# Attention and two MLP blocks on one core: narrower weights for the low half of P·V, and P·V products set between transposes

## The chip, the cores and the metric

The kernel runs on 1 core of one Trainium2 chip (trn2). The metric is the device time of one execution in microseconds (us). The kernel before takes 672.0 us (median of 3 runs, 671.81 to 672.73).

The engines are named as in the profile: PE is TensorE (matmul), PEld its weight load, DVE is VectorE, ACT is ScalarE, POOL is GpSimd, SP the engine that issues the DMAs. PE reads a stationary operand (the weights, loaded beforehand) and a moving operand from SBUF and writes to PSUM.

## The reference

An attention with a mask by hash buckets is followed by two dense blocks:

```python
mask = q_bucket[:, :, :, None] == k_bucket[:, :, None, :]       # 6 sign bits of q @ proj, k @ proj
scores = scale * np.matmul(q, k.transpose(0, 1, 3, 2))          # 2 x 8 heads, 768 x 768, head size 64
scores = np.where(mask, scores, -1000000000.0)
scores = scores - np.max(scores, axis=-1, keepdims=True)
attn = np.exp(scores)
attn = attn / (np.sum(attn, axis=-1, keepdims=True) + 1e-09)
return np.matmul(attn, v).astype(np.float32)
...
zr, zi = x * cos(x @ w_theta), x * sin(x @ w_theta)             # second block
u = x + w_tok_r @ zr + w_tok_i @ zi;  x = u + relu(u @ w_ch)
...
x + relu(layernorm(x) * g_ln @ w_ch1) @ w_ch2                   # third block
```

All is float32. The change touches the attention alone, in its product of the normalised P (`attn`) with V.

## The kernel before

**Halves.** A float32 factor is split into a high half, which PE multiplies exactly enough in its fast 32-bit form (fp32r), and a low half, the rest. A product is then made of several matmuls whose sum is accumulated in PSUM.

**Steps.** The 16 heads have 768 rows of scores each. One unit of work `p` is 256 rows of a head (two tiles of 128 rows, called a and b), so there are 48 units. For a unit the stages are:

- `Sa`, `Sb` (`s_mm`, L316): scores of tile a and b, four matmuls each, into a PSUM tile that has one buffer for a and one for b.
- `Ma`, `Mb` (`s_max`, L325): DVE takes the row maximum. `Ea`, `Eb` (`s_exp`, L343): ACT makes the exponentials p and their sums l. `R1`, `R2` (L353, L357): POOL and DVE make 1/l. `na`, `nb` (L361): POOL scales, which gives pn.
- `U0`, `U1`, `U2` (`p_transpose`, L374): PE transposes the twelve 128x128 blocks of pn, four to a PSUM bank (T0, T1, T2).
- `H0` to `H2` (L383): ACT copies a bank of four transposed blocks to pth, which rounds them to the high half. `L0` to `L2` (L101): DVE subtracts, which gives the low half ptl.
- `PV` (`pv_mm`, L399): twelve matmuls, six with pth and six with ptl as moving operand (256 columns). The weights are 128 columns of vv: the 64 columns of V's high half beside the 64 of its low half. So rows 0 to 63 of the result hold P times V high and rows 64 to 127 hold P times V low. They go to the bank `O`, of which there is one.
- `O` (`pv_evac_a`, L408): ACT copies rows 64 to 127 to ot. `X` (`pv_evac_b`, L417): DVE adds rows 0 to 63 and ot into xT. The next unit may write the bank O only after `X`.

**Order.** The order in which the instructions of each engine stand is written out by hand. The first units are in a list (`head`). From step k = 8 on, the list `plan` is gone through once a step; its number is how many units an operation lags, so step k holds `Sa` of unit k, `U0` to `U2` of unit k-2 and `PV` of unit k-3. Each engine does its part of that list in order, and waits in place where something is not ready. In four steps (k = 19 to 22) `plan_b` is used instead. It also makes the hash bits of four pairs of heads: `B1`, eight matmuls on PE (L272); `B2`, a copy on ACT (by, L288); `B3`, a comparison on DVE (bb, L294); `B4` on POOL. In `plan_b`, `U2` stands ahead of `U1`, and DVE's `X` stands behind `B3`. The text calls these the four bits steps, and the others plain steps.

`G`, `C` and `D` in the lists are places for background work of that step (splitting K, Q and V into halves, converting weights). `C` is ACT's: copies `hiq`, `hik` (L196) and `vv` (L94) of 128x384. For the V of a pair of heads, `v_steps` says in which step it is loaded and in which two steps its halves are made; POOL follows one step later with V's low half.

A last list (`tail`) holds the last units and the start of the second block.

Of the kernel before, what the change touches and what calls it, by code (L numbers as in the profile page):

```python
# [33 lines left out]
def attn_moe_kernel(  # L34
# [18 lines left out]
    NI = S // 128  # L53
# [9 lines left out]
    vec, act, pool, pe, sp = nc.vector, nc.scalar, nc.gpsimd, nc.tensor, nc.sync  # L63
# [7 lines left out]
    def bank(tag, name):  # L71
        return psum.tile([128, 512], F32, tag=tag, name=name)
# [6 lines left out]
    ident = const.tile([128, 128], F32, name="ident")  # L79
# [132 lines left out]
    vv_t = {}  # L212
# [78 lines left out]
    def bits_b_(pairs, nm, hf):  # L291
        n = pairs[0], nm, hf
        b = ap_.tile([64, HALF], F32, name="bb", **bits_tag(pairs, nm, hf))
        vec.scalar_tensor_tensor(  # L294
            out=b, in0=bits_ps.pop(n)[0:64], scalar=-1.0, in1=bits_y.pop(n), op0=ALU.mult, op1=ALU.is_lt
        )
        bits_b[n] = b

    def bits_p_(pairs, nm, hf):
        n = pairs[0]  # L300
        b = bits_b.pop((n, nm, hf))
        r0 = 0 if nm == "q" else 64
        pool.tensor_scalar(
            out=halves(bits_t[n][r0:r0 + 64], hf), in0=b, scalar1=mulb[nm], scalar2=addb[nm],
            op0=ALU.mult, op1=ALU.add,
        )

    s_ps, m_t, p_t, pn_t, l_t = {}, {}, {}, {}, {}
# [58 lines left out]
    pt_t = {}  # L367
    t_ps = {}
# [19 lines left out]

    o_ps = {}

    def pv_mm(p):
        h = p // (NI // 2)
        n, e = divmod(h, 2)
        vv = vv_t[n]
        ps = bank("O", f"o{p}")[:, 0:256]
        k = 0
        for x in pt_t.pop(p):
            for c in range(NI):
                pe.matmul(  # L399
                    ps, vv[:, c, e].rearrange("p a d -> p (a d)"), x[:, c::NI, :],  # L400
                    start=(k == 0), stop=(k == 2 * NI - 1),
                )
                k += 1
        o_ps[p] = ps

    def pv_evac_a(p):
        t = ap_.tile([64, 256], F32, tag="ot", bufs=3, name=f"ot{p}")
# [19 lines left out]
    def theta_steps(c, x):  # L427
# [18 lines left out]

    plan = (
# [3 lines left out]
    )  # L451

    plan_b = (
# [4 lines left out]
    )  # L458

# [77 lines left out]
    def at(step, fn, *args):  # L537
        bg.setdefault(step, []).append((fn, args))
# [8 lines left out]
    for h in range(5, B * H):  # L547
        at({8: 20}.get(h, 3 * h - 7), stack_dma, h)
        at({8: 21, 9: 21}.get(h, 3 * h - 7), stack_bits, h)
    v_steps = {2: (6, 9, 10), 3: (15, 16, 18), 4: (20, 22, 23)}  # L550
    for n in range(2, NPAIR):
        ld, *hi = v_steps.get(n, (6 * n - 6, 6 * n - 3, 6 * n - 2))
        at(ld, load_v, n)
# [12 lines left out]
    for i in range(8):  # L566
        c, x = divmod(i, 2)
# [31 lines left out]
    def run_bg(q):  # L599
# [10 lines left out]
        "R1": s_guard, "R2": s_recip, "na": lambda p: s_norm(p, 0), "nb": lambda p: s_norm(p, 1),  # L610
        "B1": lambda p: bits_chunk(*bq[p], "T1"), "B2": lambda p: bits_y_(*bq[p]),
        "B3": lambda p: bits_b_(*bq[p]), "B4": lambda p: bits_p_(*bq[p]),
        "PV": pv_mm, "O": pv_evac_a, "X": pv_evac_b,
    }
    for u in range(3):
        ops[f"U{u}"] = lambda p, u=u: p_transpose(p, u)
# [27 lines left out]
    def bp_(x, e):  # L644
# [20 lines left out]
        vh=lambda n, x: v_hi(n, act, x), vl=lambda n, x, e: v_lo(n, ve[e], x),  # L665
        D=direct_mm, Q=direct_bits, S=s_mm, M=s_max, E=s_exp, tb=s_lone, R1=s_guard, R2=s_recip,
        n=s_norm, U=p_transpose, H=p_hi, L=p_lo, PV=pv_mm, O=pv_evac_a, X=pv_evac_b,
    )

# [691 lines left out]
    last = """  # L1361
# [71 lines left out]
```

## Time and profile before

| | |
|---|---|
| median of 3 runs | 672.0 us (671.81 to 672.73) |
| the profiled execution | 672.49 us, its span 670.7 us |
| PE busy | 661.3 us, 99% of the span |
| DVE busy | 565.0 us, 84% |
| ACT busy | 417.3 us, 62% |
| POOL busy | 336.1 us, 50% |
| granted TensorE clock | 1.00 over the whole span |

The span runs from the first to the last instruction; the 1.8 us between it and the time of the execution lie outside the trace. The attention with its steps fills the first 240 us. Busy shares are means over stages that differ: in the attention three engines are each close to full, later PE alone is. Matmuls overlap in the records, since one starts while the results of the one before are still on their way to PSUM, so what a matmul costs PE is the distance of two starts and not its duration.

### The profile page before, as it was taken

Reading aid. Unit: us, or ns where it says so; the run is one execution under the profiler, and the core shown is the slowest. Engines: PE = TensorE matmul, PEld = TensorE weight load, DVE = VectorE, ACT = ScalarE, POOL = GpSimd, SP = SyncE. Lnnn points to the kernel's source line nnn. Section 1 sums busy time; section 2 is a strip of 40 time slices with the busy share of each in tenths; the row PEclk is TensorE's granted clock in tenths of the full one; section 3 lists DMA queues with packets and bytes.
Section 4 is the critical chain, followed back from the end, with each engine's and each line's share of the span. In section 5 each row is a group of like instructions: output and inputs, shape, how many; then the busy total and the mean of one; then the engine's idle time right before and its main releaser. Section 6 shows DMA issues by size and latency. Waiting matters only on the chain.

```text
span 670.7 us, 11175 instructions
## 1 busy us (share of the span) xinstructions
PE 661.3 (99%) x3766; PEld 590.0 (88%) x3766; DVE 565.0 (84%) x989; ACT 417.3 (62%) x865; POOL 336.1 (50%) x476
## 2 busy tenths in 40 slices
PE   8999999999999999999999999999999999999997
PEld 7899999999899888878888888988998988889896
DVE  6999988999999999999988888996766676767654
ACT  7899998999999897666534644554333434343321
POOL 6797888777887655342513445523241505050400
PEclk9999999999999999999999999999999999999999
DMA  8777554475542111121532113101111111220013
GB/s 247 189 169 208 138 115 113 95 182 134 129 114 89 48 47 64 47 82 45 172 110 80 47 56 102 63 1 64 63 64 64 64 64 63 77 82 32 0 48 141
DMA packets 32229, 62.23 MB, mean 93 GB/s; under 512 B 4466, under 2 KB 11460, under 8 KB 32173
## 3 DMA queue, kind: packets, MB, share of 16 engines
q1 hardware_dynamic: 32173, 61.53, 31.9%
q8 instruction: 30, 0.49, 0.3%
q14 instruction: 26, 0.21, 0.1%
HBM read 39.98 MB, written 3.15 MB: 64 GB/s over the span
## 4 chain that ended last, share of the span: by engine, by line
PE 82%; DVE 9%; POOL 3%; DMA 2%; issue 2%; ACT 1%; SPq 0%; DVEq 0%; POOLq 0%; ACTq 0%
PE o L1155 20%; PE zy L1120 12%; PE acc L840 11%; PE o L399 8%; PE t L374 8%; PE s L316 8%; PE v L1120 5%; PE a L882 5%; POOL pn L361 2%; DVE arena L101 1%; PE th L774 1%; DMA raws<-in_kT_dram 1%; PE bits L272 1%; DMA tk<-lok 1%; DVE cy L124 1%
## 5 line engine op out<-in xcount | busy, mean ns | idle before, releaser
L1155 PE MATMUL o<-arena,hh 128*128 128x512 f32 x384 | 119.7, 393 | 0.0
L361 POOL TENSOR_SCALAR pn<-p,l,M 128x768 f32<-128x768 f32 x96 | 95.0, 991 | 24.1 <-DVE l L357 16.8
L325 DVE TENSOR_REDUCE M<-s 128x1 f32<-128x772 f32 x96 | 91.1, 950 | 3.1 <-PE s L316 1.8
L101 DVE TENSOR_TENSOR ptl<-t,pth 128x512 fp32r<-128x512 f32 x144 | 90.7, 680 | 0.3 <-ACT pth L383 0.2
L343 ACT ACTIVATE p<-s,M 128x768 f32<-128x768 f32 x96 | 87.2, 908 | 5.7 <-DVE M L325 5.1
L383 ACT ACTIVATE pth<-t 128x512 fp32r<-128x512 f32 x144 | 81.8, 599 | 4.5 <-PE t L374 3.0
L316 PE MATMUL s<-tk,tq 128*128 128x386 f32 (+1 forms) x360 | 82.5, 351 | 0.0
L374 PE MATMUL t<-ident,pn 128*128 128x128 f32 x576 | 81.1, 274 | 1.1 <-DVE ptl L101 0.4
L1128 ACT ACTIVATE sn<-zy 128x384 f32<-128x384 f32 x48 | 23.6, 491 | 91.6 <-PE zy L1120 91.6
L1155 PEld LDWEIGHTS o<-arena,hh 128*128 128x128 f32 x384 | 70.5, 188 | 9.7 <-DVE arena L101 0.2
L1155 PE MATMUL o<-arena,hl 128*128 128x512 f32 x192 | 76.1, 397 | 0.0
L374 PEld LDWEIGHTS t<-ident,pn 128*128 128x128 f32 x576 | 67.6, 141 | 9.4 <-POOL M L332 2.5
L840 PE MATMUL acc<-arena,tokh 128*128 128x512 f32 x240 | 75.5, 395 | 0.0
L117 POOL TENSOR_SCALAR cs<-st 128x512 f32<-128x512 f32 (+2 forms) x65 | 41.4, 642 | 56.3 <-DVE cy L124 53.5
L316 PEld LDWEIGHTS s<-tk,tq 128*128 128x128 f32 (+1 forms) x360 | 59.3, 190 | 0.2 <-ACT vv L94 0.2
L1086 POOL TENSOR_TENSOR s<-cy 128x256 f32<-128x256 f32 x7 | 5.2, 742 | 96.8 <-DVE cy L124 96.8
L1145 DVE SCALAR_TENSOR_TENSOR hl<-c,hh 128x384 fp32r<-128x384 f32 x48 | 28.3, 591 | 28.3 <-ACT hh L1141 28.2
L840 PEld LDWEIGHTS acc<-arena,tokh 128*128 128x128 f32 x240 | 44.2, 188 | 8.9 <-DVE arena L101 0.3
L124 DVE SCALAR_TENSOR_TENSOR cy<-cy,cs 128x512 uint32<-128x512 uint32 (+2 forms) x72 | 43.6, 606 | 6.8 <-ACT cy L114 1.0
L114 ACT ACTIVATE cy<-st 128x512 f32<-128x512 f32 (+2 forms) x72 | 40.1, 561 | 11.7 <-DVE tokl L101 4.9
L840 PE MATMUL acc<-arena,tokl 128*128 128x512 f32 x120 | 46.9, 391 | 0.0
L121 DVE SCALAR_TENSOR_TENSOR cs<-st,cs 128x512 uint32<-128x512 uint32 (+2 forms) x76 | 46.2, 608 | 0.2
(233 smaller groups left out, 1555.8 us busy)
## 6 DMA issues: line engine op xcount, KB each, us to landing
st<-in_w_dram SPq DMA_DIRECT2D x36, 256.0 KB
st<-in_w_dram SPq DMA_DIRECT2D x14, 512.0 KB
tk<-hik SPq DMA_DIRECT2D x30, 193.0 KB
tq<-hiq SPq DMA_DIRECT2D x30, 192.0 KB
st<-in_wrT_dram SPq DMA_DIRECT2D x12, 384.0 KB
st<-in_wiT_dram SPq DMA_DIRECT2D x12, 384.0 KB
vs<-in_v_dram SPq DMA_DIRECT2D x8, 384.0 KB
tk<-lok SPq DMA_DIRECT2D x15, 193.0 KB
```

Of the source, the lines that this page charges most:

```text
L101: eng.tensor_tensor(out=o, in0=i, in1=f(hi), op=ALU.subtract)
L124: vec.scalar_tensor_tensor(out=yu, in0=yu, scalar=3, in1=su, op0=ALU.logical_shift_left, op1=ALU.bitwise_or)
L316: pe.matmul(ps[:, hf, 0:HW], lt[0:K, x * 128:(x + 1) * 128], rt[0:K, hf, :], start=(K == 128), stop=(K != 128),)
L325: vec.tensor_reduce(out=m_t[p][:, 0, i:i + 1], in_=s_ps[p, i][:, :, 0:HW], axis=AX.XY, op=ALU.max, negate=True)
L343: act.activation(pt, ps[:, :, 0:HALF], AF.Exp, bias=m[:, 0, i:i + 1], accum_out=l_t[p][:, 0, i:i + 1])
L361: pool.tensor_scalar(out=pn.rearrange("p c s -> p (c s)"), in0=p_t.pop((p, i)).rearrange("p c s -> p (c s)"), scalar1=l_t[p][:, 1, i:i + 1 ...
L374: pe.transpose(ps[:, w * 128:(w + 1) * 128], pn_t[p, i][:, c, :], ident)
L383: act.activation(ph, t_ps[p, u], AF.Copy)
L399: pe.matmul(ps, vv[:, c, e].rearrange("p a d -> p (a d)"), x[:, c::NI, :], start=(k == 0), stop=(k == 2 * NI - 1),)
L840: pe.matmul(acc, w[:, x, t * 128:(t + 1) * 128], z[:, x, y, :], start=(j == 0 and k == 0), stop=(j == NI - 1 and k == 5),)
L1120: pe.matmul(ps_t[r, b], W1[g][y][:, w, d, :], XB[s][x][:, z, d, :], start=(first == 1 and k == 0), stop=(k == 5), skip_group_check=True,)
L1155: pe.matmul(ps, lt[:, i * 128:(i + 1) * 128], W2[g][:, y, x, :], start=(k == 0), stop=(k == 5))
```

## The change

```diff
+    NARROW = 72
+    LOW, HIGH = range(NI, 2 * NI), range(NI)
+
+    def pv_one(p, k, first, last):
+        n, e = divmod(p // (NI // 2), 2)
+        y, c = divmod(k, NI)
+        m = NARROW if y else 128
+        pe.matmul(
+            o_ps[p][0:m], vv_t[n][:, c, e].rearrange("p a d -> p (a d)")[:, 0:m], pt_t[p][y][:, c::NI, :],
+            start=first, stop=last,
+        )
+        if last:
+            pt_t.pop(p)
+
     def pv_mm(p):
...
+        o_ps[p] = bank("O", f"o{p}")[:, 0:256]
+        ks = (HIGH[0], *LOW, *HIGH[1:])
+        for k in ks:
+            pv_one(p, k, k == ks[0], k == ks[-1])
+
+    def pv_rest(p):
+        ks = (*LOW[4:], *HIGH[1:])
+        for k in ks:
+            pv_one(p, k, False, k == ks[-1])
+
+    def pv_between(p):
+
+        q = p + 1
+        o_ps[p] = bank("O", f"o{p}")[:, 0:256]
+        ps = bank("T2", f"t{q}_2")
+        for k in HIGH[:1]:
+            pv_one(p, k, k == 0, False)
+        for w in range(4):
+            i, c = divmod(8 + w, NI)
+            pe.transpose(ps[:, w * 128:(w + 1) * 128], pn_t[q, i][:, c, :], ident)
+            pv_one(p, LOW[w], False, False)
+        t_ps[q, 2] = ps
...
     plan = (
-        ("R2", 1), ("U1", 2), ("Sb", 0), ("Mb", 0), ("H1", 2), ("U2", 2), ("Ea", 0), ("ta", 0), ("H2", 2),
-        ("G", 0), ("na", 1), ("PV", 3), ("tb", 0), ("Eb", 0), ("L0", 2), ("C", 0), ("L1", 2), ("O", 3),
+        ("R2", 1), ("U1", 2), ("Sb", 0), ("Mb", 0), ("H1", 2), ("PW", 2), ("Ea", 0), ("ta", 0), ("H2", 2),
+        ("G", 0), ("na", 1), ("PX", 3), ("tb", 0), ("Eb", 0), ("L0", 2), ("C", 0), ("L1", 2), ("O", 3),
...
-    v_steps = {2: (6, 9, 10), 3: (15, 16, 18), 4: (20, 22, 23)}
+    v_steps = {2: (6, 9, 10), 3: (15, 16, 17), 4: (20, 22, 23)}
...
+        "PV": pv_mm, "PW": lambda p: pv_between(p - 1), "PX": pv_rest, "O": pv_evac_a, "X": pv_evac_b,
```

A product with P's low half now has 72 weight columns: V's high half and 8 columns of its low half. In the head and the tail `pv_mm` still makes a unit's twelve products together, with the first high one ahead of the six low ones. In the 40 steps of `plan` and `plan_b`, `PW` stands in `U2`'s place: the first high product of unit k-3, then four times one transpose of `U2` (unit k-2) and one narrow low product. `PX` stands in `PV`'s place with the remaining two low and five high products. `plan_b` is edited in the same way.

PE in a plain step before: the transposes of `U2` (t_2) are followed by the products of unit k-3 (o). What stands in brackets is the engines whose semaphores an instruction waits for.

```order
L316 MATMUL s_1_937<-tk_581,tq_579 128x386 [waits PE_49,Activation_49]
L316 MATMUL s_1_937<-tk_581,tq_579 128x386
L316 MATMUL s_1_937<-tk_582,tq_580 128x386 x2
L374 MATMUL t_2_944<-ident,pn_1_923 128x128 [waits DVE_49]
L374 MATMUL t_2_944<-ident,pn_1_923 128x128 x3
L399 MATMUL o_973<-pth_860,vv_556 128x256 [waits DVE_49]
L399 MATMUL o_973<-pth_860,vv_556 128x256 x5
L399 MATMUL o_973<-ptl_861,vv_556 128x256 x6
```

The same place now:

```order
L316 MATMUL s_1_937<-tk_581,tq_579 128x386 [waits PE_49,Activation_49]
L316 MATMUL s_1_937<-tk_581,tq_579 128x386
L316 MATMUL s_1_937<-tk_582,tq_580 128x386 x2
L398 MATMUL o_944<-pth_860,vv_556 128x256 [waits DVE_49]
L425 MATMUL t_2_945<-ident,pn_1_923 128x128
L398 MATMUL o_944<-ptl_861,vv_556 72x256
L425 MATMUL t_2_945<-ident,pn_1_923 128x128
L398 MATMUL o_944<-ptl_861,vv_556 72x256
L425 MATMUL t_2_945<-ident,pn_1_923 128x128
L398 MATMUL o_944<-ptl_861,vv_556 72x256
L425 MATMUL t_2_945<-ident,pn_1_923 128x128
L398 MATMUL o_944<-ptl_861,vv_556 72x256 x3
L398 MATMUL o_944<-pth_860,vv_556 128x256 x5
```

The first product, which waits for DVE (for `X` of the unit before, which frees the bank O), now stands ahead of the four transposes instead of behind them.

PE in the second of the four bits steps, from the transposes of `U2` (t_2) on, before:

```order
L374 MATMUL t_2_1690<-ident,pn_1_1682 128x128 [waits DVE_49,Pool_49]
L374 MATMUL t_2_1690<-ident,pn_1_1682 128x128 x3
L374 MATMUL t_1_1698<-ident,pn_0_1640 128x128 [waits DVE_49]
L374 MATMUL t_1_1698<-ident,pn_0_1640 128x128
L374 MATMUL t_1_1698<-ident,pn_1_1682 128x128 x2
L399 MATMUL o_1708<-pth_1588,vv_1057 128x256 [waits DVE_49]
L399 MATMUL o_1708<-pth_1588,vv_1057 128x256 x5
L399 MATMUL o_1708<-ptl_1589,vv_1057 128x256 x6
```

And the same step now:

```order
L398 MATMUL o_1691<-pth_1588,vv_1057 128x256 [waits DVE_49,Activation_49]
L425 MATMUL t_2_1692<-ident,pn_1_1683 128x128 [waits Pool_49]
L398 MATMUL o_1691<-ptl_1589,vv_1057 72x256
...
L398 MATMUL o_1691<-ptl_1589,vv_1057 72x256
L374 MATMUL t_1_1706<-ident,pn_0_1641 128x128 [waits Activation_49]
L374 MATMUL t_1_1706<-ident,pn_0_1641 128x128
L374 MATMUL t_1_1706<-ident,pn_1_1683 128x128 x2
L398 MATMUL o_1691<-ptl_1589,vv_1057 72x256 x2
L398 MATMUL o_1691<-pth_1588,vv_1057 128x256 x5
```

Here eight transposes, those of `U2` and of `U1`, now stand behind the product that waits.

On ACT the order is the same but for one copy of vv (the second half of V's pair 3), which goes from the second bits step to the first. Before, from the by of the first bits step to that of the third:

```order
L196 ACTIVATE hiq_1558<-raws 128x384
L196 ACTIVATE hiq_1624<-raws 128x384 [waits DMAHW5_49,DMAHW0_49]
...
L288 ACTIVATE by<-bits 64x384 [waits PE_49]
...
L94 ACTIVATE vv_1556<-vs_1465 128x6x64
L196 ACTIVATE hiq_1624<-raws 128x384
```

And now:

```order
L94 ACTIVATE vv_1556<-vs_1471 128x6x64
L196 ACTIVATE hiq_1558<-raws 128x384
L196 ACTIVATE hiq_1631<-raws 128x384 [waits DMAHW5_49,DMAHW0_49]
...
L288 ACTIVATE by<-bits 64x384 [waits PE_49]
...
L196 ACTIVATE hiq_1631<-raws 128x384
```

So the first bits step has three such copies and the second has one, where each had two. On POOL the subtraction that goes with this copy comes one step earlier too. The orders of DVE and of SP's DMAs are as before.

## Rows read from the trace of the kernel before

**Rows 1.** The page, part 1: busy time (share of the span) and instructions.

```profile
PE 661.3 (99%) x3766; PEld 590.0 (88%) x3766; DVE 565.0 (84%) x989; ACT 417.3 (62%) x865; POOL 336.1 (50%) x476
```

**Rows 2.** Stretches: busy PE, PEld, DVE, ACT, POOL (counts), clock, DMA share, GB/s.

```profile
59.33:80.18 20.85, 20.85 (x163) 20.47 (x162) 20.39 (x36) 20.61 (x46) 18.77 (x31) 1.00 0.53 142
93.61:115.95 22.34, 22.34 (x163) 21.76 (x162) 18.59 (x33) 19.49 (x42) 18.21 (x28) 1.00 0.43 100
133.23:225.05 91.82, 91.17 (x672) 85.42 (x673) 90.69 (x163) 86.39 (x190) 72.24 (x117) 1.00 0.47 118
```

**Rows 3.** Timeline of PE, a plain step: start, us, what, count.

```profile
68.47 0.88 PE L399 MATMUL o<-ptl,vv 128*128 128x256 f32 x6
69.18 0.87 PE L316 MATMUL s<-tk,tq 128*128 128x386 f32 x4
69.89 1.04 PE L374 MATMUL t<-ident,pn 128*128 128x128 f32 x8
70.68 0.97 PE L316 MATMUL s<-tk,tq 128*128 128x386 f32 x4
71.48 0.60 PE L374 MATMUL t<-ident,pn 128*128 128x128 f32 x4
```

**Rows 4.** Timeline of DVE, the same step.

```profile
70.19 0.95 DVE L325 TENSOR_REDUCE M<-s 128x1 f32<-128x772 f32 x1
71.17 0.42 DVE L417 TENSOR_TENSOR xT<-o,ot 64x256 f32<-64x256 f32 x1
```

**Rows 5.** One line's matmuls: duration ns min/median/max, first and last start.

```profile
L374 PE MATMUL t<-ident,pn x576: 270/272/331, 20.9 to 242.1; 128*128 128x128 f32 x192
...
L399 PE MATMUL o<-pth,vv x288: 274/282/388, 30.2 to 248.2; 128*128 128x256 f32 x144
```

**Rows 6.** Timeline of PEld where P·V waits for X.

```profile
212.13 0.77 PEld L399 LDWEIGHTS o<-pth,vv 128*128 128x128 f32 x6 [0.27 <-DVE xT L417]
```

**Rows 7.** Timeline of DVE at that place.

```profile
211.66 0.42 DVE L417 TENSOR_TENSOR xT<-o,ot 64x256 f32<-64x256 f32 x1
...
214.84 0.95 DVE L325 TENSOR_REDUCE M<-s 128x1 f32<-128x772 f32 x1
```

**Rows 8.** Timeline of PE at that place.

```profile
213.66 0.87 PE L316 MATMUL s<-tk,tq 128*128 128x386 f32 x4
```

**Rows 9.** Timeline of PE, the four bits steps.

```profile
98.39 1.04 PE L374 MATMUL t<-ident,pn 128*128 128x128 f32 x8
...
100.69 0.86 PE L316 MATMUL s<-tk,tq 128*128 128x386 f32 x4
...
102.66 0.34 PE L272 MATMUL bits<-lok,pb_lo 128*128 128x384 f32 x1
...
103.99 1.04 PE L374 MATMUL t<-ident,pn 128*128 128x128 f32 x8
...
106.30 0.87 PE L316 MATMUL s<-tk,tq 128*128 128x386 f32 x4
...
117.46 0.87 PE L316 MATMUL s<-tk,tq 128*128 128x386 f32 x4
```

**Rows 10.** Timeline of DVE, the first two bits steps.

```profile
98.59 0.42 DVE L417 TENSOR_TENSOR xT<-o,ot 64x256 f32<-64x256 f32 x1
...
104.19 0.42 DVE L417 TENSOR_TENSOR xT<-o,ot 64x256 f32<-64x256 f32 x1
```

**Rows 11.** Timeline of ACT, from the first bits step to the second.

```profile
99.46 1.09 ACT L383 ACTIVATE pth<-t 128x512 fp32r<-128x512 f32 x2
100.43 0.94 ACT L196 ACTIVATE hiq<-raws 128x384 fp32r<-128x384 f32 x2
101.26 0.90 ACT L343 ACTIVATE p<-s,M 128x768 f32<-128x768 f32 x1
...
102.28 0.38 ACT L408 ACTIVATE ot<-o 64x256 f32<-64x256 f32 x1
103.04 0.49 ACT L288 ACTIVATE by<-bits 64x384 f32<-64x384 f32 x1 [0.38 <-PE bits L272]
```

More of the change, by code (lines that the diff above doesn't have):

```diff
@@ L389, in attn_moe_kernel @@
     o_ps = {}
-    def pv_mm(p):
[L392 to L404, printed above, removed]
+    NARROW = 72
[10 more added lines that the diff above has]
+            pt_t.pop(p)
+    def pv_mm(p):
+        o_ps[p] = bank("O", f"o{p}")[:, 0:256]
[17 more added lines that the diff above has]
+        t_ps[q, 2] = ps
     def pv_evac_a(p):
@@ L612, in attn_moe_kernel @@
         "B3": lambda p: bits_b_(*bq[p]), "B4": lambda p: bits_p_(*bq[p]),
-        "PV": pv_mm, "O": pv_evac_a, "X": pv_evac_b,
+        "PV": pv_mm, "PW": lambda p: pv_between(p - 1), "PX": pv_rest, "O": pv_evac_a, "X": pv_evac_b,
     }
```

4 rows, old and new, of the table plan_b are left out of this document.

## The prediction

> **What bounds the kernel now.** I read the page first. PE is busy for 99% of the span, DVE for 84% [rows 1]. That says that PE counts, but not where, so next come the stretches of the attention, since the change touches nothing else. In five plain steps (59.33 to 80.18) PE is busy all the time, DVE for 20.39 of 20.85 us and ACT for 20.61 [rows 2]: three engines are full at once, and one step takes 20.85 / 5 = 4.17 us. In the four bits steps PE is busy throughout, but DVE only for 18.59 of 22.34 us; a step takes 5.58 us and is PE's. From 133 to 225 us, 21 steps of 4.37 us on average, DVE has 90.69 of 91.82 us: there DVE is the bound. So PE work that is saved is worth at most DVE's idle time: 0.46 / 5 = 0.09 us a step early, 1.13 us in the whole late stretch.
>
> Then the timelines, for what a matmul costs PE. Six P·V products take 69.18 - 68.47 = 0.71 us, 0.12 each. Eight transposes and four score matmuls behind them take 71.48 - 69.89 = 1.59 us; the four score matmuls alone are 0.71 (69.18 to 69.89), so a transpose costs 0.88 / 8 = 0.11 [rows 3].
>
> **The change part by part.** *Narrow weights alone.* A P·V matmul lasts 282 ns, but 388 where nothing hid its weight load, so 128 columns load in 106 ns; for a transpose 331 - 272 = 59 ns [rows 5]. A load of 106 ns is hidden behind a product every 0.12 us. Where low products follow each other, a shorter load saves nothing: 0, and 0.12 stays. No row has a load of 72 columns. It lies between 0 and 106 ns if narrowing doesn't make it longer; I take 106 x 72/128 = 60 ns, close to the 59 of the nearest short load.
>
> The Trainium skill (TensorE: Matmul & The Clock Gate, "LDWEIGHTS (loading the stationary operand)") says that a load goes with its columns at 1.2 per ns, whatever the rows. That makes an estimate of 107 ns for 128 columns, which the 106 here agrees with, and 60 for 72; by it the sum below stands, and with a load that doesn't shrink, rival 1 would hold.
>
> *Pairs.* A transpose followed by anything with 128 weight columns costs 0.11, as if it waited for the 106 ns of the next load. With a 60 ns load behind it, the pair of transpose and low product should cost 0.06 + 0.12 = 0.18 instead of 0.11 + 0.12 = 0.23. The ends are 0.12 (the transpose vanishes) and 0.23 (the transpose itself holds PE). At 0.18, PE saves 4 x 0.05 = 0.19 us a step (0.44 - 0.25). In the head and tail nothing stands between: 0.
>
> *The wait that moves.* The bank O is free only when DVE has made xT. Before, that wait stood behind `U2`; now `U2` stands behind it, and in the bits steps `U1` too. The signal takes 212.13 - (211.66 + 0.42) = 0.05 us [rows 6, 7]. Then PE needs 0.11 for the unhidden load, 0.12 for the first product, 4 x 0.18 = 0.72, and seven more products, 0.83: 1.78 us until the next `Sa`.
>
> In a plain step this closes a loop: xT, signal 0.05, PE 1.78, `Sa` 0.87 until its result is there [rows 3], then DVE's maximum and xT, 71.59 - 70.19 = 1.40 [rows 4]: 4.10 us, and a signal from PE to DVE. In the rows DVE takes `Sa` 0.14 us after its end (70.05 to 70.19), though it was busy until then, so that signal is at most 0.14. The loop is 4.10 to 4.24 against 4.17 today. Where P·V already waits for xT there was more room: `Sa` ended at 214.53 and DVE came at 214.84 [rows 7, 8]; now `Sa` ends 1.78 + 0.05 - (213.66 - 212.08) = 0.25 later, still before 214.84. So PE's saving pays for the late start and no more: 0 a step. The ends are -0.07 and +0.07 in some 27 steps (40 less four bits steps, a third of the 21 late ones whose loop has room because DVE converts weights too, and two at the start); DVE's idle time allows no gain over 0.09 x 11 + 1.13 = 2.1 us. I carry -1 and +1.9.
>
> *The bits steps.* Here xT stands behind bb, which waits for ACT's by, which waits for eight bits matmuls. xT of the first ends at 99.01 [rows 10], while PE began `U2` at 98.39 [rows 9]. Now PE waits until 99.06. It then does the 1.78 us and, between, four transposes of `U1` (0.44): 2.22 us, so the next `Sa` starts at 101.28 instead of 100.69: +0.59. Queued behind the wait are `U2`, `U1`, the rest of P·V and the next scores, and ACT waits for `U1`. This now goes round:
> - PE's way: from `Sa` to by is 103.04 - 100.69 = 2.35, from by to the end of xT 104.61 - 103.04 = 1.57, signal 0.05, PE 2.22: 6.19 us a step instead of 5.58 [rows 9 to 11].
> - ACT's way: PE's last transpose of `U1` ends 0.11 + 0.12 + 0.72 + 3 x 0.11 + 0.27 = 1.55 after the wait; signal 0.03; two evictions 0.97 (99.46 to 100.43); copies at 0.83 / 2 = 0.415 each; from the exponential to ot 1.02; ot and the gap 0.41 [rows 11]. Then by.
>
> Second step: by PE's way by starts at 101.28 + 2.35 = 103.63. By ACT's it is 99.06 + 1.58 + 0.97 + 3 x 0.415 + 1.02 + 0.41 = 104.29, with three copies since one of vv moved here. The later counts: xT ends at 105.86, PE goes on at 105.91, where `U2` began at 103.99. Third: PE's way gives by at 105.91 + 2.22 + 2.35 = 110.48, ACT's, with one copy, 110.31; so PE goes on at 112.10. Fourth, no copies: 112.10 + 6.19 = 118.29. The next `Sa` is at 120.51 instead of 117.46: +3.05 us. Nothing gives it back, since DVE has only 1.13 us idle in the whole later stretch and its order is unchanged.
>
> *POOL and ACT for V.* The moved copy is counted above; POOL's subtraction (one of its late ones) falls where POOL has 22.34 - 18.21 = 4.1 us idle [rows 2]: 0. Uncovered it would delay only the next norm. DMAs keep their order and place.
>
> **Sum.** 0 for the weights, 0 (-1 to +1.9) for the plain steps, +3.05 for the bits steps: 672.49 + 3.05 = 675.5 us for an execution like the profiled one. That one stands 0.49 above the median of 672.0, so the forecast is 675.0 us, its own range 674.0 to 677.0.
>
> **Rivals.** 1. *The pairs bring nothing* (the load doesn't shrink, or a transpose holds PE for its 0.11 whatever follows). For it: a transpose's own load is 59 ns, yet transposes in a row still cost 0.11, so something other than that load sets their distance. Against it: eight transposes take only 0.79 until the next score matmul is let in (69.89 to 70.68), which then waits, so PE seems free sooner. Then each loop is 0.19 longer: the bits steps cost 3.05 + 4 x 0.19 = 3.8, and the 27 plain steps some 0.17 each, 4.6: 680.4 us.
>
> The Trainium skill (the same page, "Part 4: PE-mode transpose") says that transposes don't lift the clock as matmuls do and that one takes about 275 ns; the 272 here agrees, but the granted clock is 1.00 in all three stretches, so the trace doesn't say that the array is held. By that rule rival 1 would come.
>
> 2. *Not slower: the transposes vanish wholly* (a pair costs 0.12). For it speaks the same 0.79. Against it, the weights must still be in place, and no row shows a load under 59 ns. PE then needs 1.78 - 0.24 = 1.54, the plain loop is at most 4.00, and DVE's idle time becomes the gain: up to 2.1 us. The bits steps cost less: the first 0.59 - 0.24 = 0.35, then PE's `U1` ends 0.24 sooner, so 105.67, and two more of 5.95: 117.57 + 1.98 = 119.55 against 117.46, +2.1. Sum 0: 672.0 us. It decides from pairs under some 0.13 on; anything more that hides in the bits steps makes it faster.
>
> 3. *Late transposes stall others.* `H2` on ACT comes later where P·V waited for xT, by the moved wait; against it, ACT has 91.82 - 86.39 = 5.4 us idle in that stretch [rows 2]. If DVE's low halves then wait, 0.1 us in each of the 40 steps adds 4: 679.
>
> **Chances.** Forecast 0.58; rival 1 0.18; rival 2 0.17; rival 3 0.07. Under 0.2% (1.3 us) this kernel's runs can't be told from no change. Rival 2 lies around no change: same 0.11, faster 0.06. The rest is slower: 0.83. For 8 in 10 the range reaches from rival 2's 671.6 to 681.0 above rival 1: about 0.1 is left out in all.
>
> **What would show it.** In the profile after: low products with 72 columns 0.18 apart where a transpose lies between (0.23: rival 1, 0.12: rival 2); PEld waiting for xT in nearly all plain steps by 0.1 to 0.3 us, at unchanged 4.17 a step; four bits steps of some 6.0 to 6.8 us in place of 5.58, with PE idle by 0.7 us or more before each; the second with three copies the longest. DVE's idle time in the bits steps grows by 3 us. If the bits steps stay at 5.6, the forecast is wrong at its main term; if plain steps leave 4.17 by more than 0.1, at the loop.

## The result and the profile after

The changed kernel takes 680.55 us (median of four runs, 679.93 to 681.16); the kernel before took 672.07 beside it. The ratio is 1.012, with a 95% interval of 1.0108 to 1.0131: 8.5 us slower, where 3.0 were forecast. The number that came is the one of rival 1.

The page, part 1, and the chain of waits by engine (part 4), of the kernel after, then that chain of the kernel before:

```profile
PE 665.3 (98%) x3766; PEld 590.3 (87%) x3766; DVE 567.4 (84%) x989; ACT 419.0 (62%) x865; POOL 334.5 (49%) x476
...
PE 64%; DVE 21%; POOL 4%; issue 4%; ACT 4%; DMA 2%; SPq 1%; DVEq 0%; POOLq 0%; ACTq 0%
```

```profile
PE 82%; DVE 9%; POOL 3%; DMA 2%; issue 2%; ACT 1%; SPq 0%; DVEq 0%; POOLq 0%; ACTq 0%
```

The busy times hardly differ from [rows 1]: no engine has more work (PE's record has 4.0 us more, but it counts waits as busy, as seen below). What is new is waiting, and the chain now goes through DVE for 21% of the span, where it was 9%. Three stretches of the kernel after follow: five plain steps, the four bits steps and 21 late steps, each cut from one `Sa` to another (columns as in [rows 2]):

```profile
61.24:82.92 21.68, 21.68 (x163) 20.30 (x161) 21.09 (x36) 21.29 (x47) 19.18 (x31) 1.00 0.59 158
95.60:121.93 26.33, 23.61 (x162) 21.72 (x161) 18.55 (x32) 19.01 (x42) 18.63 (x28) 1.00 0.33 77
135.04:229.84 94.80, 91.78 (x675) 85.08 (x674) 92.20 (x162) 87.91 (x190) 72.80 (x119) 1.00 0.45 115
```

The stretches in [rows 2] were cut from one P·V to another. For the first two that makes 0.01 us of difference at most; the same 21 late steps of the kernel before, from `Sa` to `Sa`, are these:

```profile
129.98:222.00 92.02, 91.34 (x675) 85.44 (x673) 90.83 (x163) 86.54 (x190) 72.87 (x118) 1.00 0.46 118
```

The granted clock is 1.00 in all of them. A plain step takes 21.68 / 5 = 4.34 us, 0.17 more; the four bits steps 26.33 - 22.34 = 3.99 more, and PE is idle in them for 2.72 us, where it had no idle time; the 21 late steps 94.80 - 92.02 = 2.78 more. The rows of waits of the kernel after, 30 to 240 us (engine, line, what it waited for: total, times, longest), name the place:

```profile
PEld o L398 <- DVE xT L440: 9.7, 23, 0.8
ACT pth L383 <- PE t L374: 7.5, 11, 1.5
PE o L398 <- DVE xT L440: 5.4, 11, 1.0
ACT pth L383 <- PE t L425: 5.0, 14, 0.6
```

PEld waits for xT 9.7 us, in 23 of the 36 plain steps. Of PE's 5.4 us, 3.2 lie in eight of those same steps and are part of the 9.7; the other 2.2 are in three of the bits steps. So P·V waits for xT about 11.9 us in 26 steps. In the kernel before, that wait was 1.4 us in 6 steps, of which [rows 6] show one. One plain step, first on PE, then on DVE:

```profile
69.91 0.87 PE L316 MATMUL s<-tk,tq 128*128 128x386 f32 x4
...
72.28 0.39 PE L398 MATMUL o<-pth,vv 128*128 128x256 f32 x1
72.51 0.27 PE L425 MATMUL t<-ident,pn 128*128 128x128 f32 x1
72.54 0.36 PE L398 MATMUL o<-ptl,vv 128*72 128x256 f32 x1
72.74 0.27 PE L425 MATMUL t<-ident,pn 128*128 128x128 f32 x1
72.76 0.36 PE L398 MATMUL o<-ptl,vv 128*72 128x256 f32 x1
72.96 0.27 PE L425 MATMUL t<-ident,pn 128*128 128x128 f32 x1
...
74.24 0.87 PE L316 MATMUL s<-tk,tq 128*128 128x386 f32 x4
```

```profile
70.82 0.96 DVE L325 TENSOR_REDUCE M<-s 128x1 f32<-128x772 f32 x1
71.81 0.42 DVE L440 TENSOR_TENSOR xT<-o,ot 64x256 f32<-64x256 f32 x1
...
75.14 0.96 DVE L325 TENSOR_REDUCE M<-s 128x1 f32<-128x772 f32 x1
```

The pairs stand 72.74 - 72.51 = 0.23 us apart. A low product starts 0.03 us after its transpose, but lasts 360 ns where one without a transpose in front takes 280, as if it waited inside the array. The loop can be read off, link by link: xT ends at 72.23, PE goes on at 72.28, the next `Sa` starts 1.96 later (1.78 was forecast), DVE's maximum 0.90 after that, and the next xT ends 1.41 after the maximum starts: 0.05 + 1.96 + 0.90 + 1.41 = 4.32, and 74.24 - 69.91 = 4.33. PE counts as busy for all 21.68 us of the plain stretch, although it waits 0.15 to 0.33 us in each step: PEld shows that wait (20.30 us busy). In PE's record it is hidden, since the last score matmul ends only at 72.38, after the first product has started.

The second bits step of the kernel after, the longest. First ACT, then DVE:

```profile
101.38 1.09 ACT L383 ACTIVATE pth<-t 128x512 fp32r<-128x512 f32 x2 [1.42 <-PE t L374]
102.35 0.53 ACT L94 ACTIVATE vv<-vs 128x384 fp32r<-128x384 f32 x1
102.76 0.94 ACT L196 ACTIVATE hiq<-raws 128x384 fp32r<-128x384 f32 x2
103.59 0.90 ACT L343 ACTIVATE p<-s,M 128x768 f32<-128x768 f32 x1
...
104.60 0.38 ACT L431 ACTIVATE ot<-o 64x256 f32<-64x256 f32 x1
104.89 0.47 ACT L288 ACTIVATE by<-bits 64x384 f32<-64x384 f32 x1
```

```profile
99.07 0.42 DVE L440 TENSOR_TENSOR xT<-o,ot 64x256 f32<-64x256 f32 x1
...
106.03 0.42 DVE L440 TENSOR_TENSOR xT<-o,ot 64x256 f32<-64x256 f32 x1
```

This is ACT's way as the prediction walked it, with `U1` queued behind the wait: ACT stands for 1.42 us until PE's transposes are there, then makes three copies, and by comes so late that xT ends at 106.45 (105.86 forecast). From xT to xT this step takes 6.96 us.

### The profile page after: what moved, and what is told of

It is laid out like the page before. It is cut to its first block, busy times and chain, and to the rows that moved or that the text cites. A ratio compares the mean times of both kernels' runs of the same rounds, so it can differ in the third digit from the quotient of the medians.

```text
span 678.5 us, 11176 instructions
## 1 busy us (share of the span) xinstructions
PE 665.3 (98%) x3766; PEld 590.3 (87%) x3766; DVE 567.4 (84%) x989; ACT 419.0 (62%) x865; POOL 334.5 (49%) x476
## 4 chain that ended last, share of the span: by engine, by line
PE 64%; DVE 21%; POOL 4%; issue 4%; ACT 4%; DMA 2%; SPq 1%; DVEq 0%; POOLq 0%; ACTq 0%
PE o L1178 20%; PE zy L1143 12%; PE acc L863 11%; DVE ptl L101 5%; PE v L1143 5%; PE a L905 5%; DVE M L325 5%; PE o L398 4%; PE s L316 2%; POOL pn L361 2%; ACT p L343 2%; DVE xT L440 2%; DVE cy L124 1%; PE t L374 1%; DVE arena L101 1%
## 5 line engine op out<-in xcount | busy, mean ns | idle before, releaser
L398 PE MATMUL o<-pth,vv 128*128 128x256 f32 x288 | 53.8, 295 | 6.0 <-DVE xT L440 5.4
L398 PE MATMUL o<-ptl,vv 128*72 128x256 f32 x288 | 59.1, 327 | 0.0
L374 PE MATMUL t<-ident,pn 128*128 128x128 f32 x416 | 56.3, 273 | 0.3 <-DVE ptl L101 0.2
L398 PEld LDWEIGHTS o<-pth,vv 128*128 128x128 f32 x288 | 40.9, 189 | 15.1 <-DVE xT L440 9.7
L374 PEld LDWEIGHTS t<-ident,pn 128*128 128x128 f32 x416 | 48.5, 141 | 4.0 <-POOL pn L361 0.6
```

The source lines that it names most:

```text
L374: pe.transpose(ps[:, w * 128:(w + 1) * 128], pn_t[p, i][:, c, :], ident)
L398: pe.matmul(o_ps[p][0:m], vv_t[n][:, c, e].rearrange("p a d -> p (a d)")[:, 0:m], pt_t[p][y][:, c::NI, :], start=first, stop=last,)
```

## The experiments

Theory H: a transpose of fp32 holds the array for its 0.11 us whatever stands behind it, so pairs give nothing, and the whole cost is the wait that moved ahead of `U2`. The rivals are in the expectations. Times stand against the kernel before, run on the same chip in the same turn. Edits are shown against the kernel after, but for the last, which is against the kernel before. "Pair" is the median distance from one transpose to the next across a low product, over 120 pairs of the trace.

**Which part costs.** Five kernels each take one thing away.

The weights wide again, order of after:

```diff
-    NARROW = 72
+    NARROW = 128
```

> The changed kernel with 128 weight columns in the low products again; order unchanged. Theory H (a transpose holds PE 0.108 us whatever stands behind it, so pairs bring nothing and the moved wait is the whole cost): pairs of transpose and low product stay 0.228 us apart, 680.5 us (680 to 681). Rival L (the load still sets the pair; narrowing already saved something): the load is 106 - 60 = 46 ns longer, each step 4 x 0.046 = 0.18 us, 40 steps 7 us: about 688 us.

681.18 us, ratio 1.0121 (1.0106 to 1.0136). The pair is 0.231 (0.228 in the kernel after). Rows of that kernel's line of products, and of the same line after (duration min/median/max, first and last start):

```profile
L398 PEld LDWEIGHTS o<-ptl,vv x288: 187/189/194, 31.2 to 257.2; 128*128 128x128 f32 x144
```

```profile
L398 PEld LDWEIGHTS o<-ptl,vv x288: 140/142/148, 30.5 to 256.0; 128*72 128x72 f32 x144
```

The load does shrink by 47 ns with 72 columns (189 to 142), as the forecast took it, and it doesn't matter here: rival L is out, and so is the first half of the forecast's rival 1.

Only the weights narrow, order of before:

```diff
-        ... ("PW", 2), ... ("PX", 3), ...   (both plans)
+        ... ("U2", 2), ... ("PV", 3), ...
-    v_steps = {2: (6, 9, 10), 3: (15, 16, 17), 4: (20, 22, 23)}
+    v_steps = {2: (6, 9, 10), 3: (15, 16, 18), 4: (20, 22, 23)}
```

> Order of before (U2 and PV as they were, third V pair split in the old step), only with 72 columns in the low products. Theory H: 672.0 us (671.5 to 672.7). Rival N (72-column weights cost something themselves, a switch of the array's width): part of the 8.5 us appears here, 674 to 680 us, with low products more than 0.12 us apart.

672.22 us, ratio 0.9997 (0.9987 to 1.0007), low products 0.117 apart. The forecast's first term, 0 for narrow weights alone, stands.

The first product ahead, but transposes and low products not mixed:

```diff
         for w in range(4):
             i, c = divmod(8 + w, NI)
             pe.transpose(ps[:, w * 128:(w + 1) * 128], pn_t[q, i][:, c, :], ident)
+        for w in range(4):
             pv_one(p, LOW[w], False, False)
```

> The first product still ahead of U2, but then four transposes together and four low products together, no pairs. Theory H: the wait alone costs; four transposes 0.43 and four low products 0.48 take what four pairs took (0.91), so 680.5 us (680 to 681). Rival P (standing in pairs costs or saves): if pairs cost, 672 to 678; if they saved something, above 682.

680.10 us, ratio 1.0104 (1.0083 to 1.0125). The interval overlaps that of the full change, so pairing neither costs nor saves what can be told from these runs; putting the first product in front brings the time by itself.

The new order in plain steps only, and in bits steps only (`bq` holds the bits steps):

```diff
-        "PW": lambda p: pv_between(p - 1), "PX": pv_rest,
+        "PW": lambda p: p_transpose(p, 2) if p in bq else pv_between(p - 1),
+        "PX": lambda p: pv_mm(p) if p + 1 in bq else pv_rest(p),
```

> The new order in the plain steps only; the four bits steps and the split of the third V pair as before. Theory H: the 40 plain steps lose 0.14 to 0.17 us each except where a stall hides it: from the trace of after +3.4 us behind the bits steps and up to 1.1 ahead of them: 675.4 to 676.5 us. The forecast's account (plain steps cost nothing): 672 us.

```diff
-        "PW": lambda p: pv_between(p - 1), "PX": pv_rest,
+        "PW": lambda p: pv_between(p - 1) if p in bq else p_transpose(p, 2),
+        "PX": lambda p: pv_rest(p) if p + 1 in bq else pv_mm(p),
```

> The new order in the four bits steps only (with the third V pair split one step earlier); plain steps as before. By the trace of after the bits steps cost +4.0: 676 to 676.5 us. The forecast's term for them was +3.05: 675. Together with the plain steps alone (676.5, +4.0) a sum of +8 to +8.5 would say that the two parts add.

Plain only: 676.49 us, ratio 1.0052 (1.0037 to 1.0067), +4.0. Bits only: 676.64, ratio 1.0057 (1.0040 to 1.0074), +4.3. Together 8.3 of the 8.5: the parts add. The plain steps and the bits steps of the first, then the bits steps of the second:

```profile
62.12:83.81 21.69, 21.69 (x162) 20.31 (x161) 21.10 (x36) 21.29 (x47) 19.19 (x31) 1.00 0.62 160
96.50:118.83 22.33, 22.33 (x162) 21.75 (x161) 18.53 (x33) 19.68 (x43) 17.92 (x26) 1.00 0.39 90
```

```profile
95.31:121.69 26.38, 23.67 (x162) 21.70 (x161) 18.62 (x32) 19.02 (x42) 18.99 (x29) 1.00 0.34 79
```

21.69 is the plain stretch of after, 22.33 the bits stretch of before, and 26.38 the bits stretch of after: each part makes its stretch and leaves the other alone (the second kernel's plain steps take 4.16 us).

**Is it the wait?** Here xT is made from ot alone: rows 0 to 63 of the bank O are left out of the sum, so that DVE doesn't read that bank and ACT's ot frees it. One kernel does this in the order of before (with 72 columns), the other in the new order:

```diff
-            in0=ps[0:64], in1=t, op=ALU.add,
+            in0=t, in1=t, op=ALU.add,
```

> Order of before with 72-column low products; xT is made from ot alone (rows 0 to 63 of the P.V bank are left out of the sum), so DVE no longer reads that bank and only ACT's ot frees it. Control for the next run: about 672 us by every theory, less if DVE's addition without PSUM is shorter.

> The same xT from ot alone in the new order: the first product and the transposes behind it no longer wait for DVE. Theory H (the moved wait is the cost): within 1.5 us of the control, about 672 to 673.5 us. Rival Q (the place of the low products among the transposes, not the wait, delays ACT's evictions and with them DVE): most of the 8.5 us stays, 678 to 680 us.

Order of before: 678.82 us (678.22 to 679.29). New order: 678.52 (678.00 to 679.22). The 8.5 us between the orders are gone, as theory H says and rival Q doesn't. But both are over 6 us slower than before, a miss for both expectations of some 672 us: in the control DVE's addition takes 0.42 us in some steps and up to 1.18 in others (25.7 us for 45 of them from 30 to 240 us, 18.5 in the kernel after). So DVE was a harder bound in this pair, and in its bits steps it could hide a late PE; these runs don't tell about the bits steps. In plain steps with a short addition they do. Three such steps of the new order, behind the bits steps (their additions take 0.41, 0.41 and 0.53 us), and a place on PE in the first of them:

```profile
121.17:133.66 12.49, 12.49 (x99) 12.37 (x97) 12.27 (x22) 12.28 (x27) 8.21 (x15) 1.00 0.54 126
```

```profile
123.48 0.28 PE L398 MATMUL o<-pth,vv 128*128 128x256 f32 x1
123.60 0.27 PE L425 MATMUL t<-ident,pn 128*128 128x128 f32 x1
123.63 0.36 PE L398 MATMUL o<-ptl,vv 128*72 128x256 f32 x1
123.83 0.27 PE L425 MATMUL t<-ident,pn 128*128 128x128 f32 x1
```

A step takes 12.49 / 3 = 4.16 us, as before the change, with the pairs at 0.23 and every instruction of PE in the new place. The same three steps take 13.12 us in the kernel after (121.93 to 135.05) and 12.48 in the control. The first product lasts 0.28 where it was 0.39 in the kernel after: its load is no longer unhidden.

**What holds PE in a transpose?** pn and the identity become fp32r, and with them all transposes of P:

```diff
-            pe.transpose(ps[:, w * 128:(w + 1) * 128], pn_t[q, i][:, c, :], ident)
+            pe.transpose(ps[:, w * 128:(w + 1) * 128].bitcast(F32R), pn_t[q, i][:, c, :], identr)
...
-        pn = ap_.tile([128, NI, 128], F32, tag=f"pn{i}", bufs=2, name=f"pn{p}_{i}")
+        pn = ap_.tile([128, NI, 128], F32R, tag=f"pn{i}", bufs=2, name=f"pn{p}_{i}")
```

> The new order, but pn and the identity are fp32r, and so the transposes (this rounds P and leaves its low half out). Theory H1 (a transpose holds PE for its own fp32 data, in two passes): in one pass the pair shrinks from 0.228 to about 0.18 us, the bits steps and plain steps get 0.19 us a step back, about 675 us, the forecast's own case. Rival H2 (the hold belongs to the transpose itself, whatever the type): pair 0.228, 680 us.

> Control for the fp32r transposes: the same types (P rounded, its low half left out), in the order of before, low products 72 columns wide. In the plain steps DVE and ACT are full whatever PE does, and a bits step's PE work shrinks by 12 x 0.045 = 0.5 us if one transpose goes from 0.109 to about 0.06: 670 to 672 us. Read against it, the new order with these types (675.8) costs what the forecast said of the order (+3.05) if the difference is 3 to 4, and its own price of 8.5 if it is more.

> fp32r transposes in the new order, with 128 weight columns in the low products. If the load counts once a transpose is short, a transpose can't give way before the next 106 ns load is done: the pair goes from 0.185 to about 0.225 us and the time up by some of 40 x 0.16 us, 678 to 681 us. Rival (the load never counts): pair 0.185, 675.8 us.

New order, narrow: 675.78 us, ratio 1.0049 (1.0034 to 1.0064). Order of before, narrow: 670.63, ratio 0.9982 (0.9973 to 0.9991). New order with 128 columns: 679.74, ratio 1.0110 (1.0096 to 1.0124). One step of the new order on PE, narrow and then wide (their lines stand one lower):

```profile
72.29 0.22 PE L426 MATMUL t<-ident,pn 128*128 128x128 f32 x1
72.35 0.29 PE L399 MATMUL o<-ptl,vv 128*72 128x256 f32 x1
72.48 0.22 PE L426 MATMUL t<-ident,pn 128*128 128x128 f32 x1
72.54 0.29 PE L399 MATMUL o<-ptl,vv 128*72 128x256 f32 x1
```

```profile
72.56 0.22 PE L426 MATMUL t<-ident,pn 128*128 128x128 f32 x1
72.61 0.34 PE L399 MATMUL o<-ptl,vv 128*128 128x256 f32 x1
72.79 0.22 PE L426 MATMUL t<-ident,pn 128*128 128x128 f32 x1
72.84 0.34 PE L399 MATMUL o<-ptl,vv 128*128 128x256 f32 x1
```

A transpose in a pair is 0.22 us long in place of 0.27, and the pair 0.185 in place of 0.228, with the records of the loads as long as in the kernel after (140 and 142 ns): the hold goes with the type of the data, as H1 says and H2 doesn't. That it comes from two passes, H1's reason, no run shows. Now the load counts, as the expectation of the wide kernel had it: the pair is 0.231 with 128 columns, and the kernel 3.96 us slower than with 72. From the start of a low product's load to that of the next transpose's it is 0.13 us with 128 columns (72.56 to 72.69 on PEld) and 0.09 with 72 (72.48 to 72.57). The Trainium skill (TensorE: Matmul & The Clock Gate, "LDWEIGHTS (loading the stationary operand)") gives a load 1.2 columns per ns, which makes an estimate of 47 ns for 56 columns less; 0.231 - 0.185 = 0.046 agrees.

So a pair has two limits, which nearly coincide. The loads alone give 0.231 with 128 columns and 0.185 with 72, as the forecast reckoned (0.23 and 0.18); with fp32 transposes it is 0.228 even with 72. Narrowing lifts the first limit and leaves the second.

This is close to the forecast's own case, a pair of 0.18, and so tests the rest of its sum. The bits steps of the narrow kernel, new order and order of before:

```profile
94.94:120.20 25.26, 22.34 (x162) 20.22 (x161) 18.80 (x34) 19.23 (x43) 18.80 (x30) 1.00 0.34 81
```

```profile
94.31:116.51 22.20, 22.20 (x162) 21.06 (x161) 18.45 (x33) 19.35 (x43) 18.06 (x28) 1.00 0.39 92
```

They cost 25.26 - 22.20 = 3.06 us; the forecast had 3.05. That the two agree so closely is partly luck: with these types the transposes of `U0` and `U1` are shorter too (0.084 us apart in a row, as a median, in place of 0.109), in the control as well, which the forecast didn't have.

The whole order costs 675.78 - 670.63 = 5.15 with these types. The two runs are of different turns; by their ratios it is (1.0049 - 0.9982) x 672 = 4.5, so 3 to 4, as that expectation had it, is not ruled out. In the traces the plain steps (all but the last, which runs into the tail) take 152.1 us in the new order and 149.9 in the control, so some 2 us are there. But the control's plain steps are also 1.1 us shorter than those of the same order with fp32 transposes (150.9 in a2_narrow): half of the 2 is a gain that the new order doesn't get.

**The moved copy.** Both halves of the third V pair split earlier still, so that the second bits step has two copies:

```diff
-    v_steps = {2: (6, 9, 10), 3: (15, 16, 17), 4: (20, 22, 23)}
+    v_steps = {2: (6, 9, 10), 3: (14, 15, 16), 4: (20, 22, 23)}
```

> The changed kernel with both halves of the third V pair split one step earlier still, so that the second bits step has two copies on ACT, not three. Its step was 6.97 us in the profile, the later ones 6.42 and 6.55: if the third copy made it, it becomes about 6.55 and the whole 680.1 us. Rival (something else made the second step long): 6.97 and 680.5 us.

The second bits step falls from 6.97 to 6.56 us (from one `Sa` to the next), so the third copy made it; but the plain step that got the copy rises from 4.22 to 4.43. The time, 681.00 us (680.08 to 681.17), can't be told from 680.55; the 680.1 that was expected didn't come.

**A faster version?** DVE waits 0.9 us in a bits step, and late plain steps with a theta conversion take 4.78 us. Two conversions moved, in the order of before:

```diff
-    TS = tuple(range(22, 46, 3))
+    TS = (17, 19, 25, 28, 31, 34, 37, 40)
-        ... ("R1", 1), ("B3", 2),   (plan_b)
+        ... ("R1", 1), ("D", 0), ("B3", 2),
```

> Order of before, with two of the eight theta conversions (L121, L124 on DVE, 0.41 + 0.42 us) moved into two bits steps, where DVE waits 0.9 us a step for ACT's by. Each plain step that held one took 4.78 instead of 4.17 us: about 2 x 0.6 = 1.2 us less, 670.8 us, if DVE's wait in the bits steps is really free. Rival (ACT and POOL, which get two more operations there, become late): 672 us or more.

673.17 us, ratio 1.0012 (1.0003 to 1.0021): slower, a miss. Two rows of waits in its bits steps:

```profile
PEld t L374 <- POOL pn L361: 2.2, 3, 1.3
ACT pth L383 <- PE t L374: 2.0, 3, 1.2
```

Neither wait is in the bits steps of the kernel before. DVE had the time (20.88 of 24.17 us busy in these steps), POOL had less of it (21.36): with the conversion's POOL work in the same steps, the norms pn came late, then PE's transposes, then ACT. No version that computes all of P beat the kernel before; the fp32r control did by 0.18%, at the price of P's low half.

## Why the prediction missed

- *The step that failed* is the *Pairs* term: "With a 60 ns load behind it, the pair of transpose and low product should cost 0.06 + 0.12 = 0.18". It measured 0.228. The 60 ns were right (the load is 47 ns shorter than the 106), and so was the 0.18 as far as loads go (0.185 with fp32r transposes). The reading that a transpose costs 0.11 "as if it waited for the 106 ns of the next load" was wrong: an fp32 transpose costs that by itself, 0.109 in a row in front of loads of 59 ns, and 0.228 - 0.119 = 0.109 in pairs. The evidence lay in rows that were read: transposes in a row stand 0.11 apart though their own load is 59 ns [rows 3, 5], which the prediction put under rival 1. The 0.79 for eight of them, which weighed against it, was time until the next matmul was let in, not until the array was free: it is seven distances of 0.109 and the 0.03 us after which, in the rows of after, a product is let in behind a transpose, to last 80 ns longer.
- *Narrow weights alone, 0:* right (0.9997, 0.9987 to 1.0007).
- *Bits steps, +3.05:* 3.99 in the stretch, and 4.3 alone. The mechanism is the one that was walked through, PE's way and ACT's way included, and the size follows from the pair: rival 1 put 3.8 for a pair of 0.23, and with fp32r transposes, where the pair is 0.185, the stretch costs 3.06.
- *Plain steps, 0 (-1 to +1.9):* +4.0. The loop was right, with 0.18 us more in it: PE's part was 1.96 in place of 1.78, and 4.33 a step is above the 4.17 of DVE. (Not all of that 4.17 is DVE's own: with fp32r transposes the control has late plain steps of 3.93 us.) Rival 1's 27 x 0.17 = 4.6 was near it. With the short pair the plain steps still cost some 2 us against their control, at the upper end, and 1.1 against the same order with fp32 transposes; which link makes this rest wasn't tried.
- *Where a part of the plain steps' cost went unseen:* five of them cost 0.83 early, but the first bits step starts only 0.48 late (95.60 after, 95.12 before). PE and POOL of before and then PE of after, ahead of it:

```profile
90.19 0.86 PE L316 MATMUL s<-tk,tq 128*128 128x386 f32 x4
...
92.27 0.44 PE L374 MATMUL t<-ident,pn 128*128 128x128 f32 x2 [0.41 <-POOL pn L361]
```

```profile
88.16 0.10 POOL L189 MEMSET lok<- 128x4 f32 x1 [0.57 <-DMA tk<-lok]
```

```profile
91.38 0.88 PE L316 MATMUL s<-tk,tq 128*128 128x386 f32 x4
...
95.60 0.33 PE L316 MATMUL s<-tk,tq 128*128 128x386 f32 x1
```

  Before, one step was held up by a DMA through POOL and took 95.12 - 90.19 = 4.93 us; the later kernel meets that DMA when it is done and takes 4.22. The hold-up belongs to that execution and not to the order: in the trace of a2_narrow, with the old order, POOL doesn't wait there and the step takes 4.40. Against that trace the new order costs 4.0 us in the bits steps and 4.5 in the plain ones, 8.5 in all.
- *POOL and ACT for V:* the copy costs 0.4 us where it stands, as ACT's way counted it.
- *Rival 2* (a pair of 0.12) never came, not even in fp32r. *Rival 3*: ACT does wait for `H2` (5.0 us in 14 steps), but with the wait for the bank gone the three steps shown are 4.16 each, so there it follows from the same wait and needs no term of its own.

The Trainium skill (TensorE: Matmul & The Clock Gate, "Part 4: PE-mode transpose"), which the prediction weighed, has about 275 ns for one transpose in a kernel, of bf16 data. The fp32 rows, 270 to 272, are near it; the fp32r transposes took 222 in the pairs. Rival 1's pair came with the granted clock at 1.00, so it was not the clock that held PE.

## What to carry to other kernels

A gap that mixing instructions is to fill must be shown empty first: take the distance from start to start in a row of the same kind, beside the length of its weight load, and if the distance is longer than the load, as 0.109 is longer than 0.059 here, the load is not what sets it. An instruction that waits for another engine, put ahead of work that didn't need that wait, makes a loop; add its links up, and compare with the bound of the step, with the error of the least certain link in it. Here 0.05 us a pair decided between 4.17 and 4.33 us a step.

## What was not expected of the hardware

- Transposes of 128 columns in fp32 stand 0.109 us from start to start, though their loads take 59 ns, and a pair with a low product takes 0.228 or 0.231 us, whether that product has 72 or 128 weight columns. In fp32r a transpose of a pair lasts 0.222 in place of 0.272 us, a low product starts 0.06 behind it and lasts 0.29 instead of 0.36, and only then does the width of the weights show (0.185 or 0.231).
- DVE's addition with both operands in SBUF, in place of one in PSUM, took up to 1.18 us for 0.42. One case in the order of before, DVE and then POOL:

```profile
72.94 1.09 DVE L440 TENSOR_TENSOR xT<-ot 64x256 f32<-64x256 f32 x1
```

```profile
72.74 1.02 POOL L101 TENSOR_TENSOR vv<-vs,vv 128x384 fp32r<-128x384 f32 x1
```

  It ends 0.27 us behind POOL's subtraction, as if it had stood until that was nearly done. All 19 additions of this trace that took over 0.5 us end 0.26 to 0.28 us behind an operation of POOL. The Trainium skill (SBUF — State Buffer, "Summary: rules for kernel authors") says that an operation of DVE with two SBUF inputs and one of GpSimd that reads SBUF block each other, the later one waiting for the earlier; this case agrees for DVE as the later one.
